# Sixteen products of ones at the start of an attention and feed-forward kernel

## The chip, the core and the metric

The kernel runs on one core of one Trainium2 chip. The core has five engines that work at the same time: TensorE (PE in the profile, with its weight loads as PEld), VectorE (DVE), ScalarE (ACT), GpSimd (POOL) and SyncE (SP, which here only issues transfers). Each engine works through its own list of instructions in order, and an instruction may wait for a semaphore that another engine or a transfer raises. The metric is the device time of one execution in microseconds (us).

## The reference

The inputs are q, k and v of 4 batches with 8 heads each, 576 positions and 64 elements per head, and a vector `s` per head. The first stage is causal attention with a decay:

```python
scores = scale * np.matmul(q, k.transpose(0, 1, 3, 2))
cum = np.cumsum(np.maximum(s, 0.0), axis=-1)
bias = -(cum[:, :, :, None] - cum[:, :, None, :])
scores = np.where(causal, -1e9, scores + np.minimum(bias, 0.0))
attn = softmax(scores)            # max, exp, sum, divide
x = np.matmul(attn, v)
```

Then the heads are put side by side and go through a feed-forward layer with a gate (`x @ w_in`, a convolution of three taps, a sigmoid, `@ w_out`), a mixing of positions of rank 32 with a residual, and a second feed-forward layer (`relu(u @ w_ch1) @ w_ch2`). The output is fp32.

## The kernel before

The program is written as a list of operations, each with the engine, an assumed cost, and the buffers that it reads and writes. A planner (`Plan.order`) plays this list through with the assumed costs and latencies, picks on each engine the earliest operation in the program's order among those that are ready, and gives out the eight PSUM banks by classes (`CAPS`; the class `sc` of the scores has three at most). The instructions are then issued in that order.

The part that matters here is the very beginning. The tile `cc` receives `s` (line 451), VectorE turns it into the scaled running sum in two instructions (lines 463 and 464), and rows of it go by transfer into `qkF`, the operand tile of a head (lines 594 and 597), beside the head's q and k (line 592). VectorE has cleared `qkF` before (line 455). The mask comes by transfer into a corner of `ws`, a tile whose real content, weights, comes much later, and VectorE casts it (line 363). GpSimd clears some small tiles and the mask's empty part (lines 863, 494 and 1316).

The first work of TensorE is `products` (line 693): for head 0 four score tiles of 128 rows and 128, 256, 384 and 512 columns, in fp32. In the profile each of these products is two rows. VectorE adds the mask and takes the maximum of each tile (line 654), ScalarE takes the exponential (line 671), GpSimd multiplies by the reciprocal of the sum (line 682), and TensorE transposes the result (line 816) and multiplies it with v (line 842). The last 64 rows of two heads share a tile (line 709). Heads 0 to 7 work so, the other heads with operands split in two parts (`qkA`, `qkB`). From about 50 us on, the feed-forward products (lines 886 and 928) are laid between the heads, and from about 400 us on the second feed-forward layer runs (lines 1173 and 1273).

Of the kernel before, what the change touches and what calls it, by code (L numbers as in the profile page):

```python
# [8 lines left out]
F32 = mybir.dt.float32  # L9
# [303 lines left out]
def tile_attention_moe_mixer(  # L313
# [14 lines left out]
    nc = tc.nc  # L328
    plan = Plan(tc)


    def dve(n, fn, r, w, fast=False):
        far = st.get("late") and any(getattr(x, "pool", None) is banks for x in r)
        return plan.op("DVE", (155 if far else 70) + n * (0.52 if fast else 1.042), fn, r, w)
# [4 lines left out]
    def pool(n, fn, r, w, two=False, extra=125):  # L339
        return plan.op("POOL", ((280 if st.get("late") else 148) + n * 2.1) if two else (37 + n * 0.834 + extra), fn, r, w)  # L340

    def dma(nbytes, fn, r, w):
        return plan.op("SP", 640, fn, r, w, late=nbytes / 360)

    def dma_act(fn, r, w):

        return plan.op("ACT", 100, fn, r, w, late=1900)

    def pe(ns, fn, r, w):
        return plan.op("PE", ns, fn, r, w)  # L350
# [11 lines left out]
    def hi_dve(out, src, r, w, n):  # L362
        dve(n, lambda: nc.vector.tensor_copy(out(), src()), r, w, fast=True)
# [25 lines left out]
    def bank(cls, name):  # L389
        b = Buf(banks, None, [128, 512], F32, name, [banks.opened])  # L390
        b.cls = cls
        banks.live.append(b)
        plan.banked.append(b)
        return b
# [20 lines left out]
    def early(name, at, shape, dtype, rows=128):  # L415
        n = 1
        for x in shape:
            n *= x
        axes = " ".join("abc"[: len(shape)])

        def view(t):
            v = t[:rows, at : at + n]
            if dtype != F32:
                v = v.bitcast(dtype)
            return v.rearrange(f"p ({axes}) -> p {axes}", **dict(zip("abc", shape)))

        return Part(ws, view, name)
# [3 lines left out]
    for f in range(NF1):  # L431
        w1h[f, 0] = one(wi, f"w1h_{f}", [128, 512], F32R)
        w1l[f, 0] = one(wi, f"w1l_{f}", [128, 512], F32R)
        for n, w1x in enumerate((w1h, w1l)):
            at = f * 1024 + n * 512
# [12 lines left out]
    def cum():  # L448
        return cc()

    dma(73728, lambda: nc.sync.dma_start(out=cum(), in_=s), [], [cc])
    key = [cc]
    for t in qkFs:

        dve(2 * S, lambda t=t: nc.vector.memset(t[0:64], 0.0), [], [(t, "z"), (t, "r0"), (t, "r1")], True)
        for i in range(2):
            dma_act(
                lambda t=t, i=i: nc.scalar.dma_start(out=t[i : i + 1, i, :], in_=one_d[i, 0:1, 0, :]),
                [],
                [(t, "z")],  # L460
            )

    dve(S, lambda: nc.vector.tensor_scalar(cum(), cum(), 0.0, 8.0, ALU.max, ALU.mult), key, key, True)
    scan = dve(S, lambda: nc.vector.tensor_tensor_scan(cum(), cum(), cum(), 0.0, ALU.add, ALU.max), key, key)

    def behind(o, back=1):
        o.preds.add([x for x in plan.ops if x.eng == "PE"][-back])
# [849 lines left out]
        o.preds.add(scan)  # L1317
    hi_dve(lambda: mask[:, 384:512], lambda: mraw[:, 0:128], [mraw], [(mask, 1)], 128)
    hi_dve(lambda: mask[:, 736:800], lambda: mraw[:, 128:192], [mraw], [(mask, 2)], 64)
    dma(65536, lambda: nc.sync.dma_start(out=ident[:, 0:128], in_=ident_d), [], [(ident, 0)])  # L1320
    plan.ops[-1].preds.add(st["first"])

# [75 lines left out]
    for h in range(NH + 1):  # L1398
        b, hh = divmod(h - 1, H)
        todo = []  # L1400
        if b >= 1:
            parts = m1_parts(b - 1)
            whole = sum(w for w, t in parts)
            at, todo = 0, []
# [191 lines left out]
```

## Time and profile before

| | |
|---|---|
| median of 3 runs | 809.51 us (807.74 to 813.28) |
| the profiled execution | 810.78 us, its span 809.0 us |
| TensorE | 788.1 us busy (97%), 5300 products |
| VectorE, ScalarE, GpSimd | 59%, 58% and 22% busy |
| mean granted clock of TensorE | 0.998 |

The span is the time from the first to the last instruction in the profile; the execution's own time has 1.8 us more around it. Busy times of one engine do not add up to the span with those of others, since they overlap. A clock of 1.00 stands for 2.4 GHz, 0.50 for 1.2 GHz.

### The profile page before, as it was taken

The page shows a single profiled execution, that of the slowest core. Times are in us where ns is not written, and L with a number is a line of the kernel's source. Part 1 is how long each engine was busy: PE and PEld are TensorE (multiplying, and loading weights), DVE is VectorE, ACT ScalarE, POOL GpSimd, SP SyncE. Part 2 cuts the span into 40 slices and gives each one's busy share as a digit, 9 for nine tenths or more (in the row PEclk, how much of TensorE's full clock was granted, in tenths as well). Part 3 has the DMA queues.
Part 4 walks back from the last instruction along what each step waited for, and adds up shares of the span by engine and source line. Part 5 has one row for each costly group of instructions (what it writes and reads, how often), then busy time and mean ns, then how long its engine had stood idle before and what let it go on. Part 6 is the DMA issues. An engine that isn't in the chain of part 4 may idle for free.

```text
span 809.0 us, 15163 instructions
## 1 busy us (share of the span) xinstructions
PE 788.1 (97%) x5300; PEld 707.1 (87%) x5300; DVE 477.1 (59%) x1152; ACT 465.8 (58%) x1176; POOL 181.5 (22%) x291
## 2 busy tenths in 40 slices
PE   5889999999999999999999999999999999999998
PEld 3557798999899998999999999999998888888888
DVE  5977897636855368547888967444566232323232
ACT  4878898858868488776767545444455222222221
POOL 2554464634446245241220000000000000000000
PEclk9999999999999999999999999999999999999999
DMA  6578655554454456130226356455588363636343
GB/s 166 176 207 227 188 142 151 138 135 106 149 136 108 105 131 188 35 111 1 103 68 225 121 162 210 148 180 183 168 261 275 92 207 92 204 96 191 110 130 93
DMA packets 66309, 119.69 MB, mean 148 GB/s; under 512 B 9396, under 2 KB 34868, under 8 KB 66232
## 3 DMA queue, kind: packets, MB, share of 16 engines
q1 hardware_dynamic: 66160, 118.70, 50.7%
q8 instruction: 42, 0.69, 0.3%
q14 instruction: 35, 0.29, 0.1%
q10 hardware_dynamic: 72, 0.01, 0.0%
HBM read 68.81 MB, written 28.90 MB: 121 GB/s over the span
## 4 chain that ended last, share of the span: by engine, by line
PE 88%; DVE 4%; ACT 3%; DMA 2%; issue 1%; POOL 0%; SPq 0%; DVEq 0%; POOLq 0%
PE my L1273 24%; PE ma_A L1173 16%; PE y L928 12%; PE h L886 11%; PE ma_S L1173 6%; PE sc L693 6%; PE pt L816 5%; PE av L842 5%; DMA qkA<-t 1%; PE tp L945 1%; PE t L964 1%; DVE sc L654 1%; DMA qkF<-cc 1%; PE mh L991 1%; DVE wf_w L529 1%
## 5 line engine op out<-in xcount | busy, mean ns | idle before, releaser
L1273 PE MATMUL my<-mh,w 128*128 128x512 f32 (+1 forms) x560 | 159.1, 368 | 0.0
L1173 PE MATMUL ma_A<-u,W 128*128 128x288 f32 x960 | 137.9, 295 | 0.0
L1173 PEld LDWEIGHTS ma_A<-u,W 128*128 128x128 f32 x960 | 131.4, 188 | 0.3
L1251 ACT ACTIVATE mh<-ml 128x512 fp32r<-128x512 f32 (+1 forms) x80 | 47.1, 589 | 136.8 <-DMA ml<-ch_d 76.0
L1273 PEld LDWEIGHTS my<-mh,w 128*128 128x128 f32 x560 | 101.6, 189 | 17.6
L1254 DVE SCALAR_TENSOR_TENSOR ml<-ml,mh 128x512 fp32r<-128x512 f32 (+1 forms) x80 | 50.5, 638 | 112.6 <-ACT mh L1251 112.6
L928 PE MATMUL y<-gh,w1o 128*128 128x288 f32 x512 | 113.9, 299 | 0.1
L1273 PE MATMUL my<-ml,w 128*128 128x512 f32 (+1 forms) x280 | 103.0, 368 | 0.0
L682 POOL TENSOR_SCALAR P<-P,sm 128x128 f32<-128x128 f32 (+3 forms) x128 | 73.2, 591 | 101.3 <-DVE sm L745 86.5
L654 DVE CUSTOM_DVE_ANT_0 sc<-sc,mask 128x128 f32<-128x128 f32 (+2 forms) x144 | 69.2, 497 | 33.8 <-PE sc L693 26.1
L928 PEld LDWEIGHTS y<-gh,w1o 128*128 128x128 f32 x512 | 85.4, 188 | 0.9 <-DVE c L907 0.3
L898 DVE SCALAR_TENSOR_TENSOR c<-h,cw,c 128x288 f32<-128x288 f32 x128 | 64.3, 512 | 30.9 <-ACT c L894 29.8
L886 PE MATMUL h<-xh,w1h 128*128 128x290 f32 x256 | 79.9, 312 | 0.1
L369 POOL TENSOR_TENSOR gl<-c,gh 128x288 fp32r<-128x288 f32 x64 | 53.7, 846 | 104.0 <-ACT gh L913 89.2
L886 PE MATMUL h<-xl,w1h 128*128 128x290 f32 x256 | 76.6, 299 | 0.0
L886 PE MATMUL h<-xh,w1l 128*128 128x290 f32 x256 | 76.4, 298 | 0.0
L1187 ACT COPY s<-ma_A 128x288 f32<-128x288 f32 x96 | 38.3, 401 | 64.7 <-PE ma_A L1173 56.1
L928 PE MATMUL y<-gl,w1o 128*128 128x288 f32 x256 | 75.2, 294 | 0.0
L671 ACT ACTIVATE P<-sc,sm 128x128 f32<-128x128 f32 (+3 forms) x128 | 67.8, 533 | 5.9 <-DVE sm L654 5.4
L357 ACT COPY th<-pt 128x384 f32<-128x384 f32 (+2 forms) x128 | 63.1, 494 | 9.9 <-PE pt L816 9.0
L816 PE MATMUL pt<-ident,P 128*128 128x128 f32 x320 | 59.7, 274 | 2.3 <-ACT h L892 1.3
L1273 PEld LDWEIGHTS my<-ml,w 128*128 128x128 f32 x280 | 52.8, 189 | 8.6
(135 smaller groups left out, 1527.8 us busy)
## 6 DMA issues: line engine op xcount, KB each, us to landing
ml<-ch_d SPq DMA_DIRECT2D x64, 256.0 KB
ch_d<-s SPq DMA_DIRECT2D x64, 144.0 KB
raw_w<-w_in SPq DMA_DIRECT2D x16, 512.0 KB
raw_w2a<-w_in SPq DMA_DIRECT2D x16, 512.0 KB
raw_w2b<-w_in SPq DMA_DIRECT2D x16, 512.0 KB
t<-qk_in SPq DMA_DIRECT2D x24, 288.0 KB
qkB<-t SPq DMA_DIRECT2D x24, 288.0 KB
qkA<-t SPq DMA_DIRECT2D x24, 288.0 KB
```

Source lines behind the costliest of these rows:

```text
L357: act(n, lambda: nc.scalar.copy(out(), src()), r, w)
L369: pool(n, lambda: nc.gpsimd.tensor_tensor(out(), src(), f32(hi()), ALU.subtract), r, w, two=True)
L654: lambda: nc.vector.tensor_tensor_reduce(out=ps[:rows, :w], in0=ps[:rows, :w], in1=mask[:rows, m0 : m0 + w], scale=-0.125, scalar=3.0e38 i ...
L671: lambda: nc.scalar.activation(out(), ps[:rows, :w], ACTF.Exp, bias=low(), scale=-1.0, accum_out=total()),
L682: lambda: nc.gpsimd.tensor_scalar(t[:, :w], t[:, :w], r(), 1.0, ALU.mult, ALU.mult),
L816: nc.tensor.transpose(pt[:, o + rows - 128 : o + rows], d["P"][i][:, 128 * j : 128 * j + 128], turn)
L886: nc.tensor.matmul(ps[:, :W], lhsT=ww, rhs=xx, start=kt + n == 0, stop=kt == KT - 1 and n == 2)
L898: lambda k=k: nc.vector.scalar_tensor_tensor(c(), hh[:, k : k + HS], cw[:, 3 * f + k : 3 * f + k + 1], c(), ALU.mult, ALU.add),
L928: nc.tensor.matmul(ps[:, :HS], lhsT=ww, rhs=xx(), start=f + n == 0, stop=f == NF1 - 1 and n == 2)
L1173: nc.tensor.matmul(ps[:, :HS], lhsT=ww, rhs=uu, start=first and k == 0, stop=k == 5, skip_group_check=True)
L1254: lambda: nc.vector.scalar_tensor_tensor(ml[:, :n], raw(), 0.0, f32(mh[:, :n]), ALU.max, ALU.subtract),
L1273: nc.tensor.matmul(ys[c][dt][:, :n], lhsT=ww, rhs=xx[:, :n], start=f + k == 0, stop=f == NF2 - 1 and k == 2)
```

## The change

Three groups of products are put on TensorE's list ahead of the first score: 9, 5 and 2 products of a 128x128 tile of ones with itself, in fp32, all into one PSUM bank (`turn`, of the class `sc`) that nobody reads. Each group has a tile of ones of its own in unused columns of `ws`. The first is written by GpSimd, the other two by VectorE, each placed behind the VectorE operation that stands last in the program at that point: for the second group the running sum, for the third the second cast of the mask.

```diff
+    turn = bank("sc", "turn")
+
+    def keep_busy(count, name, at, write):
+
+        t = early(name, at, (128,), F32)
+        write(t)
+
+        def mms():
+            for _ in range(count):
+                nc.tensor.matmul(turn[:, :128], lhsT=t(), rhs=t(), start=True, stop=True)
+
+        pe(count * 300, mms, [t], [turn])
+
+    def ones_pool(t):
+        pool(128, lambda: nc.gpsimd.memset(t(), 1.0), [], [t], extra=0)
+
+    def ones_dve(t):
+        last = next(x for x in reversed(plan.ops) if x.eng == "DVE")
+        dve(128, lambda: nc.vector.memset(t(), 1.0), [], [t], True).preds.add(last)
+
+    keep_busy(9, "busy0", 1400, ones_pool)
...
     scan = dve(S, lambda: nc.vector.tensor_tensor_scan(cum(), cum(), cum(), 0.0, ALU.add, ALU.max), key, key)
+
+    keep_busy(5, "busy1", 1528, ones_dve)
...
     hi_dve(lambda: mask[:, 736:800], lambda: mraw[:, 128:192], [mraw], [(mask, 2)], 64)
+    keep_busy(2, "busy2", 1656, ones_dve)
```

On TensorE the list began, before, with the scores of head 0:

```order
L1591 UNCONDITIONAL_BRANCH [waits barrier_Pool_Activation_PE_DVE_SP_release]
L693 MATMUL sc0_0_153<-qkF_0_104 128x128 [waits DMAHW2_49,DMAHW1_49,DMAHW5_49,DMAHW0_49,DVE_49]
L693 MATMUL sc0_1_157<-qkF_0_104 128x256
L693 MATMUL sc0_2_163<-qkF_0_104 128x384
L693 MATMUL sc0_3_171<-qkF_0_104 128x512 [waits Activation_49]
L709 MATMUL sc0_4_0_177<-qkF_0_104 64x288 [waits Activation_49]
```

Now it begins with the sixteen products (`turn` is their bank, `ws` holds the ones; line 716 is what was line 693, line 732 what was 709):

```order
L1615 UNCONDITIONAL_BRANCH [waits barrier_Pool_Activation_PE_DVE_SP_release]
L462 MATMUL turn_118<-ws_106 128x128 [waits Pool_49]
L462 MATMUL turn_118<-ws_106 128x128 x8
L462 MATMUL turn_118<-ws_106 128x128 [waits DVE_49]
L462 MATMUL turn_118<-ws_106 128x128 x4
L462 MATMUL turn_118<-ws_106 128x128 [waits DVE_49]
L462 MATMUL turn_118<-ws_106 128x128
L716 MATMUL sc0_0_173<-qkF_0_104 128x128 [waits DMAHW2_49,DMAHW1_49,DMAHW5_49,DMAHW0_49,PE_49]
L716 MATMUL sc0_1_177<-qkF_0_104 128x256
L716 MATMUL sc0_2_183<-qkF_0_104 128x384
L716 MATMUL sc0_3_191<-qkF_0_104 128x512 [waits Activation_49]
L732 MATMUL sc0_4_0_197<-qkF_0_104 64x288 [waits Activation_49]
```

The first score now stands behind all three groups and waits for TensorE itself where it waited for VectorE; everything behind it keeps its order. On VectorE, at the start of its list, stood:

```order
L455 MEMSET qkF_129 64x1152
L463 TENSOR_SCALAR cc<-cc 32x576
L464 SCALAR_TENSOR_TENSOR cc<-cc 32x576
L363 CAST mask<-ws 128x128
L363 CAST mask<-ws 128x64
L654 ISA sc_0_153,sm_159<-sc_0_153,mask 128x128
```

and now:

```order
L476 MEMSET qkF_139 64x1152
L484 TENSOR_SCALAR cc<-cc 32x576
L485 SCALAR_TENSOR_TENSOR cc<-cc 32x576
L471 MEMSET ws 128x128
L363 CAST mask<-ws 128x128
L363 CAST mask<-ws 128x64
L471 MEMSET ws 128x128
L677 ISA sc_0_173,sm_179<-sc_0_173,mask 128x128
```

Two small memsets are added, one ahead of the mask's casts and one behind them (line 677 is what was 654). GpSimd has one more memset, as the first of its list after the constants; the lists of ScalarE and SyncE are the same as before.

## Rows read from the trace of the kernel before

**Rows 1.** Windows: busy us of each engine (instructions), clock, DMA share, GB/s.

```profile
core 0: us, PE busy (x) PEld busy (x) DVE busy (x) ACT busy (x) POOL busy (x), PEclk, DMA share, GB/s
...
12.04:112.00 99.96, 90.52 (x592) 65.77 (x593) 81.93 (x232) 86.05 (x242) 53.79 (x73) 0.98 0.67 189
112.00:600.00 488.00, 487.51 (x3682) 463.69 (x3680) 316.22 (x789) 321.91 (x833) 126.39 (x200) 1.00 0.48 138
```

**Rows 2.** Chain that ended last, from 7.4 us: start, length, what.

```profile
7.47 4.57 PE sc L693 x8
...
12.06 0.70 DVE sc L654
```

**Rows 3.** Timeline of TensorE in narrow windows: start, us, instruction, idle before.

```profile
7.47 0.77 PE L693 MATMUL sc<-qkF 128*128 128x128 f32 x2 [7.47 <-DMA qkF<-cc]
...
8.03 0.63 PE L693 MATMUL sc<-qkF 128*128 128x256 f32 x1
...
8.88 0.85 PE L693 MATMUL sc<-qkF 128*128 128x384 f32 x1
...
10.16 1.86 PE L693 MATMUL sc<-qkF 128*128 128x512 f32 x2
...
11.96 0.46 PE L709 MATMUL sc<-qkF 128*64 128x288 f32 x2
...
13.08 0.38 PE L693 MATMUL sc<-qkF 128*128 128x128 f32 x1
...
13.08 0.49 PE L693 MATMUL sc<-qkF 128*128 128x128 f32 x2
...
15.29 1.12 PE L693 MATMUL sc<-qkF 128*128 128x512 f32 x2 [0.26 <-ACT p L671]
```

**Rows 4.** Timeline of the start, all engines.

```profile
0.73 0.10 POOL L863 MEMSET xh<- 128x2 f32 x1 [0.29 <-POOLq L1585]
...
1.04 1.02 DVE L455 MEMSET qkF<- 64x1152 f32 x1 [1.04 <-PEq L1585]
...
3.61 1.35 DVE L464 TENSOR_TENSOR_SCAN cc<-cc 32x576 f32<-32x576 f32 x1
...
6.80 0.33 DVE L363 CAST mask<-ws 128x128 bf16<-128x128 f32 x2 [1.85 <-DMA ws<-mask_in]
...
8.93 0.19 ACT L671 ACTIVATION_READ_ACCUMULATOR P<-sc,sm 128x1 f32 x1
```

**Rows 5.** Groups of instructions by shape: count, busy us, mean ns.

```profile
L363 DVE CAST mask<-ws 128x64 bf16<-128x64 f32 x1 | 0.2, 189 | 0.0
...
L494 POOL MEMSET p<- 128x64 f32 x2 | 0.2, 152 | 0.0
```

**Rows 6.** Windows with the transfers' rate, 7 to 16 us.

```profile
7.00:12.00 5.00, 4.53 (x10) 2.32 (x10) 1.60 (x8) 2.98 (x7) 0.00 (x0) 1.00 0.77 210
12.00:16.00 4.00, 3.62 (x17) 1.71 (x16) 3.36 (x15) 2.62 (x10) 1.37 (x4) 1.00 0.83 262
```

**Rows 7.** Transfers issued in the first 30 us: count, size of one.

```profile
raw_w<-w_in SPq DMA_DIRECT2D x5, 512.0 KB
qkF<-qk_in SPq DMA_DIRECT2D x5, 288.0 KB
vr<-vP_in SPq DMA_DIRECT2D x3, 320.0 KB
```

**Rows 8.** Timeline of TensorE where head 2 begins.

```profile
18.61 0.46 PE L693 MATMUL sc<-qkF 128*128 128x128 f32 x2
```

**Rows 9.** Chain that ended last: its longest transfer before 112 us.

```profile
67.38 6.99 DMA qkA<-t
```

**Rows 10.** Windows around an idle stretch and the stretch of lower clock.

```profile
54.60:56.80 2.20, 0.01 (x1) 0.00 (x0) 0.37 (x3) 1.34 (x3) 2.20 (x5) 1.00 0.93 226
...
84.00:86.60 2.60, 0.70 (x6) 0.43 (x5) 2.45 (x7) 2.42 (x7) 2.07 (x4) 1.00 0.82 248
86.70:90.30 3.60, 3.60 (x18) 2.56 (x19) 2.06 (x5) 3.24 (x10) 1.56 (x3) 0.53 1.04 246
```

## The prediction

> **What bounds the kernel now.** I read the busy time by stretch first [rows 1]. From 112 us on TensorE is the bound: it is busy for 487.5 of the 488 us up to 600 us, so what is won or lost before 112 us reaches the end unchanged. Before that it idles twice: 7.47 us until its first score [rows 3], and 9.4 us (99.96 - 90.52) between 12.04 and 112 us, where VectorE (81.9 of 100 us) and ScalarE (86.1) are nearly as full and transfers are waited for.
>
> The chain of waits comes next [rows 2]. A small transfer of operands lands, then from 7.47 us the four scores of head 0 on TensorE take 4.57 us, then VectorE and ScalarE take over. So those 4.57 us lie on the path. The timeline of TensorE shows why they are so long [rows 3]. The products start at 7.47, 8.03, 8.88 and 10.16 us: 0.56 us for the two rows of 128 columns, 0.85 for those of 256, 1.28 for those of 384, which is 0.21 us for each row and 128 columns beyond the first. At 13.08 us the second row of 128 columns adds 0.11 us (0.49 - 0.38); the pair of 512 columns takes 1.86 us at 10.16 us and 1.12 us at 15.29 us. That is a factor of two a column: until about 11.9 us, just ahead of the row at 11.96 us, TensorE ran at 1.2 GHz, then at 2.4. The clock column says 1.00 from 7 us on [rows 6]; it seems to have no record before the first change, and here the rows' pitch has to be read instead. The rise came 4.4 us after TensorE's first product, and it was busy without a break in between.
>
> A second stretch at the lower clock is recorded: 0.53 from 86.7 to 90.3 us [rows 10]. Before it TensorE had been busy for 0.70 of 2.60 us. It rose again 3.6 us later, TensorE being busy throughout. An idle stretch of 2.2 us at 54.6 us brought no fall [rows 10].
>
> **The change part by part.**
>
> *First group, 9 products.* GpSimd's memset of ones now stands where the one at 0.73 us stood. Its price lies between the 0.15 us of a 128x64 memset [rows 5] and twice that for twice the columns; I take 0.2, since even 128x2 costs 0.10 us [rows 4]. The tile is there by about 1.0 us, when the engines pass their starting barrier (VectorE starts at 1.04 us, released by TensorE's sequencer [rows 4]). TensorE is idle then, so the group costs nothing itself. At the low clock a product is two rows of 0.21 us, so nine take 3.9 us, to about 5.0. GpSimd's other memsets slide by 0.2 us; the mask among them is first read after 8.2 us, by VectorE.
>
> *Second group, 5 products.* VectorE's memset of 128 columns starts when the running sum ends, at 4.96 us [rows 4]. Price: 0.11 us by columns of the 1.02 us for 1152 [rows 4], 0.19 us by the nearest small instruction [rows 5]; I take 0.15, halfway. It is covered: VectorE idles 1.85 us until the mask lands. The products start at 5.2 us and last to 7.3 at the low clock, less if it rises.
>
> *Does the clock rise in time?* TensorE is then busy from 1.1 us with gaps of about 0.2 us. With the delay of 4.4 us [rows 3] it rises at 5.5 us, with 3.6 us [rows 10] at 4.7. The second group then ends near 6.4 us, and TensorE is idle about 0.9 us until the third; 2.2 us of idle time brought no fall at 54.6 us.
>
> *Third group, 2 products.* This one is on the path. It waits for a memset behind the casts, which end at 7.13 us [rows 4]: 7.28 us with the same 0.15, and products from 7.31. Two products are four rows: 0.49 us for the first two, 0.11 for each more [rows 3], so they end at 8.02 us at the high clock. The first score, which began at 7.47 us, now waits for TensorE itself to be through, and starts at 8.05 us instead of 7.47: 0.58 us late. If the wait costs nothing beyond the order, it starts when the last of the rows has been taken in, 0.28 us late at best; at the low clock the four rows take 0.77 + 2 x 0.21 = 1.19 us, 1.05 us late.
>
> *The four scores.* At the high clock their steps are half of 0.56, 0.85 and 1.28 us, and 1.12 us for the last: 0.28 + 0.43 + 0.64 + 1.12 = 2.47 us instead of 4.57, a gain of 2.10. The fourth score waits for ScalarE to be through with the first one's tile. Before, ScalarE ended at 9.12 us [rows 4], 0.88 us after the end of the product at 8.24 [rows 3]. Now that would be 8.05 + 0.49 + 0.88 = 9.42 us, and the fourth score is due at 9.40: no new wait to speak of.
> So VectorE gets the fourth tile at 10.54 us instead of 12.06 [rows 2]: **a lead of 1.5 us**. With the bounds of the delay it is 1.8 at best, and minus 1.05 where the clock has not risen. What follows on the chain there is work of VectorE and ScalarE, which only shifts.
>
> *What could be late next.* Head 2's q and k are fetched when head 0's tile is free, so this transfer moves 1.5 us forward too, into a busy stretch. From 7 to 16 us the transfers moved 5 x 210 + 4 x 262 = 2.1 MB [rows 6]; what was issued early (two `vr`, two `raw_w`, one `qkF`, and small things) is 2.0 MB and a little [rows 7]. So head 2's operands lie in SBUF by about 16 us even if they come last, and its score, at 18.6 us before [rows 8], would want them at 17.1. The Trainium skill ("Trainium Kernel Development and Optimization", Key Constraints) says that transfers from all queues run on the same 16 engines and interleave. By that rule the early operands could be slowed by the one brought forward, and the lead be eaten; the bytes in these rows leave about a microsecond to spare, so I keep that as a rival rather than in the sum.
>
> **The sum.** The profiled execution (810.78 us) would come to 809.3 us with 1.5 us less. It stands 1.27 us above the median of the runs shown, 809.51 us, so I forecast **808.0 us** for the median. The lists of all engines are otherwise unchanged, so nothing large can come from another order.
>
> **The rivals.**
>
> *The lead is eaten before 112 us (0.20): 809.5 us.* For it: 9.4 us of idle time of TensorE [rows 1] and waits for transfers on the chain, up to 6.99 us long [rows 9]. Against it: such a transfer is issued when an engine frees or fills a tile, so it moves with the lead.
>
> *The lower clock at 86.7 us does not come back (0.12): 806.2 us.* It costs half of 3.6 us on a path that was TensorE's there, 1.8 us [rows 10]. What went before is 0.70 us of work in 2.60; a little less idle time could be enough. Against it: this stretch waits for VectorE and GpSimd, which shift along.
>
> *A second such stretch (0.08): 809.8 us.* The same 1.8 us on the other side, taken from 808.0, if another idle stretch, such as the one at 54.6 us [rows 10], grows.
>
> *Slower: the clock is not up when the first score starts (0.10): 810.6 us.* Either the rise takes longer than the 6.9 us between 1.1 and 8.0 us, or the idle time ahead of the third group brings it down again, or products of ones do not raise it, in which case the change does not do what it says. Then the four scores run as before and start up to 1.05 us late. Against it: delays of 4.4 and 3.6 us in the rows, and 2.2 us of idle time without a fall. The Trainium skill ("TensorE: Matmul & The Clock Gate", Part 1) says that the number of slow products at the start differs from run to run of one kernel; by that rule, the one delay seen here is a sample, and this chance is not nil. No run here shows it yet.
>
> **How the numbers follow.** The forecast has 0.50, the rivals 0.20, 0.12, 0.08 and 0.10. The cases reach from 806.2 to 810.6 us; three runs of one kernel spread from 1.8 us below to 3.8 us above their median, so I widen by about 1 us on each side: 805.0 to 811.5 us. The kernel's own spread is 0.7%, so about 1%, or 8.1 us, is what a measurement can tell from no change. No case comes near that, since all that the change touches is 4.57 us of the path and 1.8 us of clock: within 1% 0.96, and 0.02 on either side for what the rows do not show.
>
> **What would show it.** Right: rows of the sixteen products from about 1.1 us with a pitch that falls from 0.21 to 0.11 us before 7 us; the first score near 8.0 us; the second row of 128 columns 0.11 us behind the first; VectorE on the fourth tile near 10.5 us; TensorE saturated some 1.5 us sooner. Wrong: the first score with a pitch of 0.21 us, or beginning after 8.5 us; the fourth tile at 10.5 us but the same time by 112 us; a stretch of lower clock elsewhere.

## The result: 0.55% slower, and the profile after

The changed kernel took **814.31 us** (median of 16 runs, 807.91 to 819.44); the kernel before, run beside it, 809.33 us (16 runs). The ratio is 1.0055, with an interval of [1.0034, 1.0077]. So the time is within 1%, but 6.3 us from the forecast and on the other side of 809.33. The execution profiled took 818.06 us (span 816.2, mean clock 0.991), 3.75 us above its median (818.06 - 814.31); the kernel before was profiled 1.45 us above its own (810.78 - 809.33). The places are therefore read from this profile, the sizes from medians and from the repeat below.

The local part first. Timeline of TensorE in the changed kernel, start and length in us:

```profile
0.99 5.86 PE L462 MATMUL turn<-ws 128*128 128x128 f32 x28 [0.99 <-POOL ws L467]
...
7.20 0.71 PE L462 MATMUL turn<-ws 128*128 128x128 f32 x4 [0.35 <-DVE ws L471]
```

Timeline of VectorE, the first of the two new memsets and the fourth score tile:

```profile
4.93 0.17 DVE L471 MEMSET ws<- 128x128 f32 x1
...
10.56 0.70 DVE L677 CUSTOM_DVE_ANT_0 sc<-sc,mask 128x512 f32<-128x512 f32 x1 [0.36 <-PE sc L716]
```

The first score starts at 7.97 us (chain below), the four scores take 2.56 us instead of 4.57, and VectorE has the fourth tile at 10.56 us instead of 12.06 [rows 2]. The lead of 1.5 us is there.

Then the chain of waits of the changed kernel:

```profile
7.97 2.56 PE sc L716 x8
...
12.88 8.57 DMA qkF<-cc
...
21.58 0.76 PE sc L716 x2
...
47.79 2.24 PE av L865 x20
...
65.41 2.24 PE av L865 x20
...
71.52 8.54 DMA qkA<-t
...
82.49 3.17 PE av L865 x20
...
102.25 2.21 PE av L865 x20
```

and the same pieces of work in the chain of the kernel before:

```profile
43.03 2.24 PE av L842 x20
...
61.27 2.24 PE av L842 x20
...
94.97 2.21 PE av L842 x20
```

A row of 2.2 KB for head 2, issued at 12.88 us, landed at 21.45 (12.88 + 8.57). Head 2's first score started at 21.58 us; before, it started at 18.61 without a wait that the profile lists [rows 8]. So by then the lead of 1.5 us has become 3.0 us of lateness. The difference is 4.8 us at the 20 products of `av` at 43.03 us, 4.1 at those of 61.27, and 7.3 at those of 94.97. The span is 7.2 us longer: behind these products nothing more is lost in this execution.

Timeline of TensorE in the changed kernel at head 2's first score; the bracket is the idle time before it and what ended it:

```profile
21.58 0.76 PE L716 MATMUL sc<-qkF 128*128 128x128 f32 x2 [4.42 <-DMA qkF<-cc]
```

Windows of the changed kernel (columns as in [rows 1]; the last three are the granted clock, the transfers' share and GB/s):

```profile
18.00:20.00 2.00, 0.00 (x0) 0.00 (x0) 0.00 (x0) 0.36 (x1) 1.64 (x3) 0.88 0.98 238
20.00:22.00 2.00, 0.42 (x2) 0.45 (x3) 0.00 (x0) 0.00 (x0) 0.00 (x0) 0.50 0.25 83
...
22.00:26.00 4.00, 4.00 (x13) 3.00 (x13) 2.23 (x8) 2.10 (x7) 0.00 (x0) 0.50 0.01 3
26.00:27.00 1.00, 1.00 (x4) 0.33 (x3) 0.76 (x2) 1.00 (x4) 0.00 (x0) 0.83 0.06 16
...
81.00:84.00 3.00, 3.00 (x14) 2.04 (x14) 1.85 (x8) 1.50 (x6) 0.00 (x0) 0.50 0.82 262
...
95.00:98.00 3.00, 3.00 (x15) 2.49 (x13) 1.45 (x4) 2.69 (x8) 2.20 (x3) 0.50 1.00 230
```

TensorE, idle since 17.16 us (21.58 - 4.42), fell to 1.2 GHz: 0.88 in the window of 18 to 20 us is half a microsecond of it, so from 19.5, and 0.83 in that of 26 to 27 is a third of one, so to 26.3. From 21.58 on it then worked 4.7 us at half speed, which can cost up to half of that; the 3.0 us of lateness have become 4.8 at 43 us. Two more such stretches lie near 82 and 96 us, where the kernel before had one [rows 10]. One follows the wait for `qkA`, now 8.54 us instead of 6.99 [rows 9]: 1.55 us for the wait and 1.7 for the stretch that is one more bring 4.1 to about 7.3. This second part belongs to this execution: it is not there in the repeat below.

What hides this on the profile's page: from 112 to 600 us both kernels are the same, and TensorE is busy 98% of the span. Window of the changed kernel, against [rows 1]:

```profile
112.00:600.00 488.00, 487.58 (x3682) 463.57 (x3681) 318.10 (x797) 324.69 (x844) 130.98 (x205) 1.00 0.48 136
```

### The profile page after: what moved, and what is told of

It reads as the page before. It is cut to its first block, busy times and chain, and to the rows that moved or that the text cites. A ratio compares the mean times of both kernels' runs of the same rounds, so it can differ in the third digit from the quotient of the medians.

```text
span 816.2 us, 15230 instructions
## 1 busy us (share of the span) xinstructions
PE 796.3 (98%) x5332; PEld 714.6 (88%) x5332; DVE 477.2 (58%) x1154; ACT 466.0 (57%) x1176; POOL 180.5 (22%) x292
## 4 chain that ended last, share of the span: by engine, by line
PE 90%; DMA 3%; ACT 3%; DVE 3%; issue 1%; SPq 0%; POOL 0%; DVEq 0%
PE my L1296 24%; PE ma_A L1196 16%; PE y L951 12%; PE h L909 11%; PE sc L716 6%; PE ma_S L1196 6%; PE av L865 5%; PE pt L839 5%; DMA qkF<-cc 2%; PE tp L968 1%; DMA qkA<-t 1%; PE t L987 1%; PE mh L1014 1%; DVE sc L677 1%; DMA ws<-mask_in 1%
```

## The experiments

The theory: the lead lets head 2's three transfers (q and k, and two rows of 2.2 KB) be issued sooner, at a moment when three larger ones are still under way: two loads of feed-forward weights (`raw_w`, 512 KB each) and the second load of v (`vr`, 320 KB); in the changed kernel they land from 14.83 to 19.71 us. There they land later than if they had been issued later. TensorE runs dry and its clock falls. The rivals: a cost of the sixteen products themselves, the clock alone, the weights or the `vr` alone, or a loss that has nothing to do with the moment of issue. Lists of SyncE, issue times in us: the kernel before (the last row is head 2's first),

```profile
9.31 0.43 SPq L539 DMA_DIRECT2D raw_w<-w_in  x1
13.17 0.51 SPq L592 DMA_DIRECT2D qkF<-qk_in  x1
```

and the changed one, where the first two rows are head 2's first and last, the next head 3's first:

```profile
11.69 0.51 SPq L615 DMA_DIRECT2D qkF<-qk_in  x1
...
12.88 0.59 SPq L622 DMA_DIRECT2D qkF<-cc  x1
14.94 0.50 SPq L615 DMA_DIRECT2D qkF<-qk_in  x1
...
17.18 10.01 SPq L562 DMA_DIRECT2D raw_w<-w_in  x2
```

**The changed kernel once more**, no edit.

> The changed kernel once more, for a second profile of the same instructions. Theory (the lead of 1.5 us brings head 2's operands into a busy stretch of transfers, and they land late): head 2's first score waits for its operands for over 1 us again, the clock falls near 20 us, median 812 to 816 us. Rival (the late landing in the first profile was one bad execution, and the time is lost elsewhere): no wait of that kind in this profile, and still 812 to 816 us.

Measured: 814.52 us, ratio 1.004 [1.0018, 1.0063]. The same wait in this kernel's timeline, 3.95 us, and the end of the same pieces in its chain:

```profile
20.93 0.76 PE L716 MATMUL sc<-qkF 128*128 128x128 f32 x2 [3.95 <-DMA qkF<-cc]
```

```profile
98.39 2.21 PE av L865 x20
```

The wait for head 2 repeats. What the first profile lost behind it does not: here the lateness is 3.4 us at these products (98.39 - 94.97), and 3.4 in the span (812.4 - 809.0). One of the 12 runs had a mean clock of 1.000 and took 807.84 us, as did one of the first 16 (807.91). Those two times are the forecast's, but neither execution was profiled, so whether its mechanism held there is not shown. The others, from 0.991 to 0.998, took 809.82 to 819.44.

**The lead taken away, the products kept.** The third group has nine products instead of two, so that the first score starts about where it did before.

```diff
-            for _ in range(count):
+            for _ in range(count + more):
...
-    keep_busy(2, "busy2", 1656, ones_dve)
+    keep_busy(2, "busy2", 1656, ones_dve, more=7)
```

> Nine products in the third group instead of two, so that the first score starts near 9.5 us and the four scores end near 12.0 us at the high clock, as before the change; the list of every engine is otherwise that of the changed kernel. Theory (it is the lead that does the harm): no lead, head 2's operands are issued near 13.2 us, its first score starts at 18.6 to 19 us without a wait over 0.5 us, median within 1.5 us of before (808 to 811 us). Rival (the sixteen products themselves, or the earlier rise of the clock, cost the time): still 812 to 816 us.

Measured: 810.53 us, ratio 1.0013 [0.9994, 1.0031]. Head 2's transfers were issued from 13.27 us on, and its score, in this kernel's timeline, shows no wait:

```profile
18.63 0.48 PE L716 MATMUL sc<-qkF 128*128 128x128 f32 x2
```

More products of ones, and no loss clear of the noise: the products are not what costs; the lead is.

**A part of the lead taken away.** The same edit with `more=3`.

> Five products in the third group instead of two: half of the lead (0.8 to 0.9 us) is left, and head 2's operands are issued near 12.4 us. Theory (the earlier the issue, the more is ahead of it): a wait between 0.5 and 3 us, median 810.5 to 813 us, between the changed kernel and the one with nine. Rival (a threshold: transfers that meet the weights at all are late): a wait of 3 us or more and 813.5 us or more.

Measured: 815.04 us, ratio 1.0057 [1.0037, 1.0076]; head 2's transfers were issued from 12.03 us on. Its timeline:

```profile
21.19 0.77 PE L716 MATMUL sc<-qkF 128*128 128x128 f32 x2 [3.68 <-DMA qkF<-cc]
```

The lead left was larger than I had meant, 1.1 us by the issue (13.17 - 12.03). The time is the rival's: no less harm than with the whole lead. The landing is near 21 us for an issue at 11.69 or 12.03, and before 18.6 for one at 13.17 or 13.27; whether it drops in a step between them or along a slope, these four kernels don't say.

**The weights held back.** The second `raw_w` is issued behind head 2's three transfers, everything else as changed.

```diff
+        if h == 2:
+            plan.ahead = plan.ops[-1]
...
+        if name == "w1_1_0":
+            plan.held = load
...
-            for o in self.order():
+            seq = self.order()
+            seq.remove(self.held)
+            seq.insert(seq.index(self.ahead) + 1, self.held)
+            for o in seq:
```

> The changed kernel with one transfer moved on SyncE's list: the second load of 512 KB of weights is issued behind head 2's three operand transfers, not ahead of them. Theory in its narrower form (head 2's operands are slowed by the weights ahead of them): they land by 16.5 us, its first score starts near 17.1 us, the lead reaches 112 us, median 807 to 809 us. Rival (the lateness comes from what is issued behind them, head 3's operands and the third weights): the wait stays at 3 us or more, 812 to 816 us.

Measured: **808.61 us**, ratio 0.9978 [0.9958, 0.9997], the lowest median of all. Its timeline and its chain:

```profile
17.06 0.49 PE L723 MATMUL sc<-qkF 128*128 128x128 f32 x2
```

```profile
41.54 2.24 PE av L872 x20
...
58.67 2.24 PE av L872 x20
...
64.79 6.52 DMA qkA<-t
...
90.59 2.21 PE av L872 x20
```

Head 2's score starts at 17.06 us, where the prediction wanted it (17.1), with no wait. The lead is still 1.5 us at 41.54; it is 2.6 at 58.67 (61.27 - 58.67) and 4.4 at 90.59 (94.97 - 90.59). Part of the growth is the stretch of lower clock of the kernel before [rows 10], up to half of its 3.6 us; here no clock fell before the end. Only 3.0 us of the 4.4 reach the end (809.0 - 806.0 by the spans): from 592.22 us on a transfer of 3.70 us stands on this kernel's chain, and behind it the lead is 3.0.

**The same move without the products of ones.** The edit of the last experiment, in the kernel before.

> The kernel before, with the same move of the second load of weights behind head 2's operand transfers, and without the sixteen products. Theory: without the lead head 2's operands are in time anyway, so nothing is gained, 808.5 to 810.5 us. Rival (the order of these transfers is worth something by itself): 807.5 us or less, or, if the weights come late now, 811 us or more.

Measured: 808.96 us, ratio 0.9982 [0.9963, 1.0]. Its chain:

```profile
43.03 2.24 PE av L849 x20
...
59.03 2.24 PE av L849 x20
```

So the 0.35 us between the two medians is all that the products are seen to bring, less than these intervals can tell from nothing. The chains show where their lead goes: 1.5 us at 41.54 against 43.03, 0.4 us at 58.67 against 59.03. Between the two the chain with the lead waits for a transfer of `qkF`, and the chain without it does not. Whether the order of the transfers gains anything by itself is not shown either: the median is 0.60 us below the 809.56 beside it, the interval ends at 1.0, and up to 43.03 us this chain is that of the kernel before.

**The `vr` held back instead.** The same move with the second `vr` (320 KB), in the changed kernel.

```diff
+        if h == 2:
+            plan.held = plan.ops[-1]
```

> The changed kernel with the second load of v (320 KB), not the second load of weights, issued behind head 2's operand transfers. Theory (what counts is the bytes that are still ahead when head 2's transfers are issued at 11.7 us): fewer bytes ahead, by three fifths of what the move of the 512 KB took away, so the wait shrinks from 4 us to 1 to 2.5 us, median 810 to 813 us. Rival (the weights' transfer is what slows them, whatever the bytes): the wait stays at 3.5 us or more and the median at 813.5 us or more.

Measured: 813.37 us, ratio 1.0037 [1.0012, 1.0063]; timeline, and a window in which the clock falls:

```profile
19.11 0.77 PE L723 MATMUL sc<-qkF 128*128 128x128 f32 x2 [1.97 <-DMA qkF<-cc]
```

```profile
18.00:19.00 1.00, 0.00 (x0) 0.00 (x0) 0.00 (x0) 0.49 (x1) 1.00 (x3) 0.65 0.36 97
```

The wait is halved as expected; the time is not. The clock still fell, during a wait of 2.0 us.

**The wait filled.** 18 products of ones stand just ahead of head 2's first score, to keep TensorE busy while it would wait.

```diff
+        fill = h == 2 and w == 128
...
+            for _ in range(18 if fill else 0):
+                o = st["ones"]()
+                nc.tensor.matmul(ps[:rows, :w], lhsT=o, rhs=o, start=True, stop=True)
```

> The changed kernel with 18 more products of ones on TensorE just ahead of head 2's first score, into the bank that this score then overwrites; they last 3.9 us at the high clock and fill the wait for head 2's operands. Theory (of the 5 us lost, a good half is the lower clock that follows the idle wait, since 4.7 of its 6.8 us lie on work that the chain waits for): the score starts at 21 to 21.6 us as before, no fall near 19 us, and the median comes 2 to 3 us down, to 811 to 812.5 us. Rival (the wait itself is nearly all of the loss): 813.5 us or more.

Measured: 813.09 us, ratio 1.0031 [1.001, 1.0052]. Timeline and windows:

```profile
17.36 4.29 PE L719 MATMUL sc<-ws 128*128 128x128 f32 x36
21.48 0.39 PE L721 MATMUL sc<-qkF 128*128 128x128 f32 x2
```

```profile
20.00:26.00 6.00, 6.00 (x44) 4.62 (x43) 3.95 (x12) 3.77 (x12) 0.00 (x0) 1.00 0.09 35
```

The clock stays at 1.00, so it was the idle time that brought it down. Against the repeat this saves 1.4 us of median, less than I expected, and the intervals overlap. The median lies between the theory's 812.5 and the rival's 813.5; 3.3 us of loss are left (813.09 - 809.75), so the lateness itself looks like the larger part. When head 2's operands landed can't be seen in these rows, since the filling ends about where the wait did; the table further below has it, at 21.11 us.

**The transfers issued later, the lead on the engines kept.** A transfer of 16 bytes, which needs head 0's reciprocals, stands ahead of head 2's three on SyncE's list.

```diff
+    gap = early("gap", 1784, (4,), F32)
+    plan.small = Op("SP", 0, lambda: nc.sync.dma_start(out=gap()[0:1], in_=plan.gate_src[0:1, 8:12]), 0, 0)
...
+            at = seq.index(self.gate) + 1
+            seq[at:at] = [self.small, *self.three]
```

> The changed kernel, with one transfer of 16 bytes put on SyncE's list just ahead of head 2's three transfers. It reads head 0's reciprocals, which VectorE ends at 12.93 us, and so holds the three back to about 13.6 us instead of 11.7, while the lead on the engines (first score 8.0 us, fourth tile 10.56 us) stays. Theory (what hurts is that head 2's transfers are issued into the transfers issued from 8.5 us on; issued later, they meet fewer of them, as in the kernel before, where an issue at 13.2 landed by 18.6): they land by 17.5 to 19.5 us although issued 1.9 us later, the score waits 0 to 2 us instead of 4.0 to 4.4, no clock fall near 19 us, median 808 to 811 us. Rival (the moment of issue decides nothing; the bytes ahead and the later start add up): landing at 21.5 to 23 us, a wait of 4.5 to 6 us, the clock falls, median 814 to 817 us.

Measured: 811.45 us, ratio 1.0032 [1.0003, 1.0061]. SyncE's list, the chain, and TensorE:

```profile
13.89 0.53 SPq L620 DMA_DIRECT2D qkF<-qk_in  x1
```

```profile
15.10 3.08 DMA qkF<-cc
```

```profile
18.31 0.46 PE L723 MATMUL sc<-qkF 128*128 128x128 f32 x2 [1.02 <-DMA qkF<-cc]
```

Issued 2.2 us later than in the changed kernel, head 2's operands landed 3.3 us earlier (18.18 us against 21.45). This is the paradox of the theory, shown with the lead in place. The median is just above what I wrote. The wait of about a microsecond that is left is part of it, and its chain has a wait for `qkA` again, 8.20 us from 66.20 on; what else is was not tried.

**More lead.** The weights held back, and the third group left out.

```diff
-    keep_busy(2, "busy2", 1656, ones_dve)
```

> The changed kernel without the third group (its memset and two products) and with the second load of weights behind head 2's operand transfers. The first score starts at 7.5 us, the clock having risen before, so the lead is near 2.1 us. Theory: head 2's operands are issued near 11.1 us and land by 16.5 us, no wait over 0.5 us, median 0.5 us below that of the version with the third group, 807.5 to 808.5 us. Rival (with more lead the operands are late again, or the idle time of 1 us ahead of the first score brings the clock down): 809.5 us or more.

Measured: 811.41 us, ratio 1.0001 [0.9979, 1.0024]. A miss. Head 2 began at 16.82 us without a wait for its operands, but the chain of this kernel has

```profile
64.76 8.62 DMA qkA<-t
...
75.34 3.70 PE av L872 x20
```

where the 20 products of `av` take 3.70 us instead of 2.24, at the lower clock for most of it. The lead met the next transfer.

**Both held back.** The second `raw_w` and the second `vr` behind head 2's three.

```diff
+            for o in (self.held, self.held2):
+                seq.remove(o)
+                seq.insert(seq.index(self.ahead) + 1, o)
```

> The changed kernel with both large transfers, the second load of weights (512 KB) and the second load of v (320 KB), issued behind head 2's three transfers. Theory (head 2's operands are late because these two are on the same engines): landing before 17 us, the score at about 17 us with no wait, no clock fall near 19 us, median 807 to 809 us, like the kernel that moves the weights alone (808.61). Rival (as without the third group, where the wait for a transfer came back at 65 us): what is held back lands late in its turn, a wait of 2 us or more appears for v or the weights before 60 us, median 810 to 813 us.

Measured: 810.42 us, ratio 1.0014 [0.9993, 1.0036]. Head 2's part came as the theory says (its score at 16.98 us, no wait), the median as the rival has it, though not by the rival's way: no wait for `vr` or weights is on its chain, but again that for `qkA`,

```profile
65.28 8.10 DMA qkA<-t
...
93.94 2.21 PE av L875 x20
```

against one of 6.52 us where the weights alone were held. Up to 41.5 us these two kernels agree (41.47 and 41.54), and at 59 us they are 0.5 us apart; most of the 3.3 us between them (93.94 - 90.59) arises from `qkA` on.

## Why the prediction was wrong, step by step

- **The three groups, right.** The memset on GpSimd took 0.20 us as estimated, those on VectorE 0.17 (estimated 0.15). The first two groups end at 6.85 us (0.99 + 5.86), ahead of the 7.3 that the low clock would have given. The third group and the first score stand where they were put, at 7.20 (7.31) and 7.97 us (8.05).
- **The clock and the four scores, right.** 2.56 us against 2.47 forecast, and 2.55 to 2.58 in every profile with products of ones, so the slower rival, a clock not up in time, did not come.
- **The lead, right:** 1.5 us at the fourth tile.
- **"What could be late next", wrong, and this is the step that failed.** It added up bytes: all that was issued up to head 2's operands has moved by about 16 us, "about a microsecond to spare". They landed at 21.45 us. The bytes had gone by: from 7 to 16 us the changed kernel moved 5 x 191 + 2 x 331 + 2 x 189 KB = 2.0 MB by the windows below, and 2.3 MB by 18 us, more than the 2.0 MB and a little that the step counted. But head 2's last row wasn't among them. By its landing about 2.9 MB had moved (2.3 + 2 x 0.238 + 2 x 0.083 from the windows shown first), 0.8 MB more than the step counted, and that is about as much as head 3's q and k (288 KB, issued at 14.94 us) and a load of weights (512 KB, at 17.18) together: transfers issued later went through beside it. A sum of bytes gives a landing time only if transfers are served in the order of issue, and nothing in the rows showed that. The kernel before could have warned me: by its trace head 2's operands landed at 18.48 us, not at 16, and its score began at 18.61. There was no microsecond to spare. The Trainium skill ("Trainium Kernel Development and Optimization", Key Constraints) says that transfers of all queues run on the same 16 engines and interleave. This trace has the like within one queue, that of SyncE: by the bytes, those 0.8 MB of later transfers had gone by before head 2's last row landed. I had set that rule aside on the strength of the byte count.
- **"Such a transfer moves with the lead", wrong.** This was the argument against the rival "the lead is eaten". The issue moved with the lead, from 13.17 to 11.69 us; the landing moved the other way, from 18.48 to 21.45. That rival had the place right and the price wrong: it ended at the time before, since I let a transfer eat the lead but not more. So nothing in the forecast reached above 811.5 us. Two of its own signs of being wrong are in the profile: the fourth tile at 10.5 us without an earlier 112 us, and a stretch of lower clock elsewhere.
- **The clock as a second price, left out.** 2.2 us of idle time without a fall [rows 10] made me count an idle stretch at its own length. The clock fell during a wait of 4.42 us, and in one kernel during one of 1.97, and the work behind it paid again; so the length of the wait alone does not tell. The rival "a second such stretch" had 1.8 us for it; the profile shows three stretches, one of 6.8 us.
- **"Reaches the end unchanged", right here and not in general.** The changed kernel kept its 7.2 us from 112 us to the end. With the weights held back a lead of 4.4 us had become 3.0 at the end.

Windows of the changed kernel, against the byte count; the last two columns are share and GB/s:

```profile
7.00:12.00 5.00, 4.75 (x22) 2.42 (x22) 2.90 (x12) 3.46 (x9) 0.00 (x0) 1.00 0.70 191
12.00:14.00 2.00, 1.64 (x6) 0.89 (x6) 1.57 (x10) 1.47 (x9) 0.88 (x3) 1.00 0.92 331
14.00:16.00 2.00, 1.28 (x6) 0.51 (x5) 1.47 (x6) 1.83 (x7) 1.91 (x3) 1.00 0.93 189
16.00:18.00 2.00, 1.16 (x9) 0.92 (x9) 1.34 (x4) 2.00 (x6) 0.42 (x2) 1.00 0.84 157
```

and of the kernel with the weights held back:

```profile
14.00:16.00 2.00, 1.29 (x6) 0.53 (x6) 1.45 (x6) 1.83 (x8) 1.92 (x3) 1.00 0.70 209
16.00:18.00 2.00, 2.00 (x15) 1.70 (x16) 1.73 (x6) 2.00 (x6) 0.39 (x2) 1.00 0.77 220
```

The changed kernel's transfer engines are busier and move less: 203 and 187 GB/s for a full share (189 / 0.93, 157 / 0.84) against 299 and 286 (209 / 0.70, 220 / 0.77). This is the stretch in which head 2's operands fall behind.

Why does an issue at 12.03 us land near 21 us and one at 13.27 before 18.6? The transfers may share the engines in turn, so that what is issued behind holds back what is ahead. Or the engines fall out of step, and a transfer ends with its slowest part. The traces record more than the views above: each of these transfers raises its semaphore in sixteen steps, and it has landed with the last. Times in us, one profile of each kernel; in the first seven the second `raw_w` is issued at 9.2 to 9.5 us:

| kernel | head 2's first issue | second `raw_w`: ninth step, last | head 2's last row: ninth step, last |
|---|---|---|---|
| changed, once more | 11.52 | 15.66, 20.01 | 17.70, 20.80 |
| wait filled | 11.55 | 15.97, 19.71 | 17.88, 21.11 |
| changed | 11.69 | 15.27, 19.71 | 17.72, 21.45 |
| `more=3` | 12.03 | 16.20, 19.61 | 18.05, 21.05 |
| before | 13.17 | 14.70, 17.47 | 16.99, 18.48 |
| `more=7` | 13.27 | 14.72, 17.70 | 17.23, 18.49 |
| transfers issued later | 13.89 | 14.54, 16.40 | 17.70, 18.18 |
| weights held back | 11.72 | issued behind head 2 | 15.40, 15.79 |

Both readings are at work. Where head 2 is issued by 12.03 us, the last step of the load of weights ahead of it comes 1.9 to 3.6 us later than where it is issued from 13.17 us on, though that load itself was issued within 0.3 us of the same time: what is issued behind does hold back what is ahead here. And in the changed kernel nine of the sixteen steps of head 2's last row were there at 17.72 us, the last 3.7 us later; with the weights held back the same two times are 0.4 us apart. The transfer waits for its slowest part.

What stays open: why some of the sixteen parts fall behind when that load of weights is ahead, and why two kernels with the same start to 41.5 us differ at `qkA`.

## What to carry to other kernels

Before bringing work forward, list the transfers whose issue moves with it and ask what they will then share the engines with; here a sum of bytes gave about 16 us for a landing that came at 18.48 before the change and at 21.45 after it. If the lead runs into such a transfer, look at the order of the queue: here one load of weights moved behind three transfers of head 2 turned 814.31 us into 808.61. That is no proof that the products of ones pay: the same move without them gave 808.96. Price a wait on TensorE twice, once for its length and once for the clock behind it.

## What the hardware showed that I had not expected

- A transfer of 2.2 KB took 8.57 us from issue to landing among others, and 3.08 us when issued 2.2 us later.
- The transfers' engines gave 187 to 203 GB/s for a full share in the changed kernel between 14 and 18 us, and 277 and 297 in the one that issued head 2's transfers later. Windows of that kernel:

```profile
14.00:16.00 2.00, 1.38 (x5) 0.61 (x5) 1.54 (x6) 1.83 (x8) 2.00 (x4) 1.00 0.52 144
16.00:18.00 2.00, 1.20 (x9) 0.97 (x9) 1.38 (x4) 2.00 (x7) 0.32 (x2) 1.00 0.63 187
```

- The runs of one kernel differ by the clock they are granted: with the weights held back, 8 of 12 runs had a mean of 1.000 and took 805.34 to 809.32 us; of the changed kernel's 28 runs two had. Whether the clock is the cause there or follows from waits that differ between runs was not tried.
